# Loads of p and of two weights over other queues, and all steps in a new order

## Chip, core and metric

The kernel runs on one core of a Trainium2 chip. A core has five engines that each work through a list of instructions of their own, in order: TensorE (PE; its weight loads are listed as PEld), VectorE (DVE), ScalarE (ACT), GpSimd (POOL) and SyncE (SP), which only issues DMAs here. DMAs issued from SP, ACT and GpSimd go into queues that the same 16 DMA engines serve. The metric is the device time of one execution in microseconds. Before the change three runs gave a median of 108.91 us (108.64 to 110.49).

## What is computed

Two attentions through a packed set of 32 queries per head, and a token mixer behind them. B = 8 batches, H = 8 heads, S = 576 tokens, head width 64, D = 512; everything comes and goes in float32.

```python
def _attn_ref(q, k, v, p):
    def sm_attn(qq, kk, vv):
        s = scale * qq @ kk.T;  a = softmax(s)
        return a @ vv
    p_packed = sm_attn(p, k, v)           # 32 packed rows per head
    return sm_attn(q, p_packed, p_packed) # 576 rows per head

def _moe_ref(x, w_q, w_k, w_out):         # x: (8, 576, 512)
    wq = x @ w_q;  wk = x @ w_k           # 64 columns each
    W_tok = scale * einsum('bsd,btd->bst', wq, wk)
    mixed = einsum('bst,btd->bsd', W_tok, x)
    return maximum(mixed, 0) @ w_out
```

## The kernel before

Each batch goes through the same chain of steps, and the steps of several batches overlap. The program has no loops over time: `ORDER` is one long list of steps, written out, and since every engine runs its instructions in program order, the list fixes the order on each engine (and the order of the DMAs on each queue). A step is written `NAME.batch.part@engine=banks`: `@V`, `@A`, `@P`, `@S` choose VectorE, ScalarE, GpSimd or SyncE where a step can run on several; the numbers behind `=` are PSUM banks. Steps of TensorE carry no letter.

The loads, `LD.x` (`load`, lines 158 to 182): `LD.kN`, `LD.qN`, `LD.vN` bring in a batch's k, q, v from the GpSimd queue, float32 to bf16 on the way (v in two DMAs). `LD.g0` and `LD.h0` are the halves of batch 0's k. `LD.P0` to `LD.P3` are the four quarters of p, 32 partitions each, loaded in float32 into `p32`; `LD.W0`, `LD.W1` are w_q and w_k in float32; `LD.O` is w_out. k, q and v have four buffers each.

At the start: `SET.*` fill constants (line 190; `pz0` zeroes `pblk`, `v0` to `v3` write the columns of ones beside v, `warm` is the operand of the warm-up matmuls, `aT`, `mask`, `idf`, `aff`, `idb` are pads, a mask and the identity). `PC` (236) casts p to bf16, `PX` (239) transposes it, `PB.0.c` (243) copies a quarter into the block layout `pblk` that S1 of batches 0 and 1 reads. `WC.1`, `WC.0` (247) cast the weights. `WARM.n` runs n matmuls on a constant.

A batch b: `KT` (254) transposes k; `S1` (262) scores of p against k; `X1` (286) the exponential; `TE` (294) transposes it (batches 2 to 7); `PV` (299) times v and ones; `RC`, `PP`, `PT` (311 to 323) divide by the sum and transpose the packed rows; `QK` (325), `QKE`, `QD` put them through w_k and w_q; `QV.b.0/1/2` (345) transposes q in three pieces; `S2.b.c` (358) scores of q; `X2` (371) the exponential; `RS` (386), `RR` (392) sums and reciprocals; `AM.b.c` (397) multiplies, part 3 being 1024 columns and part 2 256; `AT`, `AE` (405, 412) transpose through PE and copy back; `WKQ`, `WE` (424, 447), `GM`, `GE` (452, 461), `Y`, `YE` (464, 472), `MX`, `MR` (479, 485) are the mixer; `RL`, `RLF`, `RLR` (506 to 515) the relu; `OT` (518) the last matmul with w_out, four parts of 512 columns and a part 4 for two batches' remaining rows; `OE`, `OEF` (536, 539) copy it out of PSUM; `ST`, `STF` (545, 563) store it from SP or ACT. `HOLD.q7` (557) is a tiny DMA on SP that waits for q7 and so keeps the stores behind it back. `HA` (381) adds the two halves of X2's result on GpSimd, so that RS has half as much to sum; no batch uses it before the change.

Names as in "S2.5" mean the step of batch 5.

Of the kernel before, what the change touches and what calls it, by code (L numbers as in the profile page):

```python
# [33 lines left out]
QKE.3@V QV.4.0@V RL.2.1@A LD.v5 LD.k6 AM.3.3@P QD.3@P LD.q6 PV.4.0=2,3 PV.4.1 RC.4.0@V RC.4.1@V
PP.4.0@V PP.4.1@V PT.4@V AT.3.3=6 RL.2.0@A OE.1.0@A AE.3.3@A AE.3.2@V OT.2.2=0,1 S2.4.2=2,3
S2.4.3=4,5 X2.4.2@A X2.4.3@A KT.5.2@V RS.4.4@V WKQ.3.0=6,7 WKQ.3.1 WKQ.3.2 OT.2.3 WE.3.2@A
S1.5=4,5,2,3 OT.2.0=6,7 OE.2.1@A RR.4.4@V GM.3=0 OT.2.1 X1.5.1@A X1.5.0@A GE.3@A AM.4.2@V Y.3=0
QK.4=4 AT.4.2=5 YE.3@A MR.3=0,1 MX.3.1=2,3 QKE.4@A RLR.3@A LD.v6 AM.4.3@P QD.4@P LD.k7 AT.4.3=4
OE.2.0@A RL.3.1@A QV.5.1@V TE.5.1@V TE.5.0@V QV.5.2@V PV.5.0=0,1 PV.5.1 QV.5.0@V AE.4.3@V
WKQ.4.0=6,7 AE.4.2@V RC.5.1@V RC.5.0@V WKQ.4.1 WKQ.4.2 PP.5.0@V PP.5.1@V MX.3.0=4,5 WE.4.2@A PT.5@V  # L40
RL.3.0@V S2.5.3=0,1 S2.5.2=2,3 GM.4=6 OT.3.4=7 X2.5.3@A GE.4@A X2.5.2@A Y.4=6 OEF.3.4@A QK.5=0
KT.6.2@V YE.4@V S1.6=2,3,4,5 RS.5.4@V OT.3.2=6,7 QKE.5@A X1.6.1@A X1.6.0@A MX.4.0=4,5 MX.4.1=0,1
MR.4=2,3 OT.3.3 QV.6.2@V TE.6.0@V RR.5.4@V TE.6.1@V QV.6.0@V QV.6.1@V LD.q7 LD.v7 QD.5@P AM.5.2@P
AM.5.3@P RLR.4@A RL.4.0@A RL.4.1@A OE.3.1@A OT.3.0=2,3 PV.6.0=4,5 PV.6.1 RC.6.0@V RC.6.1@V PP.6.0@V
PP.6.1@V OT.3.1 AT.5.3=0 PT.6@V S2.6.2=6,7 AE.5.3@V KT.7.2@V S2.6.3=4,5 OE.3.0@A X2.6.2@A X2.6.3@A
RS.6.4@V AT.5.2=1 AE.5.2@A OT.4.2=2,3 WKQ.5.0=6,7 S1.7=4,5,0,1 WKQ.5.1 WKQ.5.2 OT.4.3 X1.7.0@A
X1.7.1@A WE.5.2@A HOLD.q7 OT.4.0=4,5 OE.4.1@A GM.5=6 OT.4.1 RR.6.4@V AM.6.3@P AT.6.3=2 QV.7.1@V
TE.7.1@V TE.7.0@V AM.6.2@V QV.7.2@V AT.6.2=3 AE.6.3@V AE.6.2@V QV.7.0@V GE.5@A QK.6=6 Y.5=7
PV.7.0=0,1 PV.7.1 OE.4.0@A QKE.6@A YE.5@A QD.6@P MR.5=4,5 MX.5.1=6,7 RC.7.0@V RC.7.1@V RLR.5@A
WKQ.6.0=2,3 ST.1.4 ST.3.4 RL.5.1@A PP.7.0@V PP.7.1@V PT.7@V WKQ.6.2 WKQ.6.1 S2.7.2=0,1 WE.6.2@V  # L50
X2.7.2@A RS.7.2@V S2.7.1=4,5 MX.5.0=6,7 S2.7.0=0,1 GM.6=2 OT.5.4=3 X2.7.1@A X2.7.0@A GE.6@A Y.6=1
QK.7=2 RR.7.2@V AM.7.2@P AT.7.2=0 OEF.5.4@A QKE.7@A AE.7.2@A YE.6@A RL.5.0@V OT.5.0=6,7 MR.6=0,1
MX.6.1=4,5 MX.6.0=2,3 RLR.6@A RS.7.0@V RR.7.0@V RS.7.1@V RR.7.1@V AM.7.1@V RL.6.1@V AM.7.0@P QD.7@P
RL.6.0@A OT.5.1 OT.5.2=0,1 AT.7.0=2 AT.7.1=3 OT.6.0=4,5 AE.7.0@V AE.7.1@V OE.5.0@V WKQ.7.0=2,3
WKQ.7.2 WKQ.7.1 WE.7.1@A WE.7.0@V OT.5.3 OE.5.1@V GM.7=2 OT.6.1 GE.7@A ST.0.0 ST.0.1 ST.2.0 ST.1.1
ST.1.0 ST.4.0 ST.3.1 ST.3.0 ST.2.1 ST.4.1 ST.5.4 ST.5.0 OE.6.0@A ST.5.1 ST.6.0 Y.7=2 YE.7@V
OT.6.2=6,7 MX.7.1=0,1 MR.7=2,3 MX.7.0=4,5 RLR.7@V RLF.7.1.0@A RLF.7.1.1@A OT.6.3 OE.6.1@A
# [6 lines left out]
def kernel(  # L64
# [11 lines left out]
    nc = tc.nc  # L76
# [11 lines left out]
    B, H, S, Dh = q.shape  # L88
# [3 lines left out]
    P = 128  # L92
# [65 lines left out]
    def load(x, eng):  # L158
        a, b = x[0], x[1:]
        if a in "gh":  # L160
            i = "gh".index(a)
            nc.gpsimd.dma_start(k_in[0][:, i], pairs(k, 0)[:, i])
        elif a == "P":
            c = int(b)
            src = p.rearrange("b (i c) (y l) d -> c (b i) y (l d)", i=2, y=2)
            (nc.sync if eng == "S" else nc.scalar).dma_start(p32[quarter(c)], src[c])
        elif a == "W":
            w = (moe_w_q, moe_w_k)[int(b)].rearrange("(i c j e) m -> (c j) i (e m)", i=2, c=4, e=2)
            (nc.sync if eng == "S" else nc.scalar).dma_start(w32[:, int(b)].rearrange("a i e m -> a i (e m)"), w)
        elif a == "O":  # L170
            nc.gpsimd.dma_start(wout, moe_w_out.rearrange("(j a) n -> a j n", a=P))
        elif a == "v":
            b = int(b)
            for i in range(2):
                src = v[b, 4 * i:4 * i + 4].rearrange("c (g r) d -> g c (r d)", r=R)
                nc.gpsimd.dma_start(v_bufs[b % NL][halves(i), 1:5], src)  # L176
        elif a == "k":
            b = int(b)
            nc.gpsimd.dma_start(k_in[b % NL], pairs(k, b))  # L179
        else:  # L180
            b = int(b)
            nc.gpsimd.dma_start(q_in[b % NL], pairs(q, b))  # L182
# [40 lines left out]
    pbf = T["o"][NO - 4].rearrange("a t n -> a (t n)")[:, 0:L * Dh // 4].bitcast(bf16)  # L223
    warm = T["o"][NO - 5].rearrange("a t n -> a (t n)")[:, 0:256].bitcast(bf16)
    p32 = T["o"][NO - 1].rearrange("a t n -> a (t n)")[:, 0:L * Dh // 2]
# [8 lines left out]
        nc.vector.transpose(o, i)  # L234

    def PC(eng, bk):
        copy(eng, pbf, p32)

    def PX(eng, bk):
        blocks(pT.rearrange("a u (y l) e -> a (u y l e)", y=2).bitcast(u32).rearrange("a (u l) -> a l u", l=L // 2),  # L240
# [322 lines left out]
    def STF(b, t, eng, bk):  # L563
        q = nc.scalar if eng == "A" else nc.sync
        q.dma_start(orows(b)[:, :, t * D:(t + 1) * D], T["o", b][:, t])

    steps = dict(PC=PC, PX=PX, WC=WC, PB=PB, KT=KT, S1=S1, X1=X1, TE=TE, PV=PV, RC=RC, PP=PP,
                 PT=PT, QK=QK, QKE=QKE, QD=QD, QV=QV, S2=S2, X2=X2, HA=HA, RS=RS, RR=RR, AM=AM,
                 AT=AT, AE=AE, WKQ=WKQ, WE=WE, GM=GM, GE=GE, Y=Y, YE=YE, MX=MX, MR=MR, RL=RL, RLF=RLF,
                 RLR=RLR, OT=OT, OE=OE, OEF=OEF, ST=ST, STF=STF)  # L570

    with tc.manual_schedule():
        for item in ORDER.split():
            name, _, bk = item.partition("=")
            name, _, eng = name.partition("@")
# [43 lines left out]
```

## Time and profile before

One execution was profiled. Its time was 108.63 us; its span, from the first to the last instruction, is 106.9 us, and what lies around it is 1.73 us.

| | |
|---|---|
| median of three runs | 108.91 us |
| profiled run: time, span | 108.63, 106.9 us |
| granted TensorE clock, mean | 0.99 |
| TensorE busy | 95.9 us, 71 of 1535 matmuls are warm-up |
| VectorE, ScalarE, GpSimd busy | 79.3, 67.6, 44.3 us |
| GpSimd queue (q0): bytes, share of the 16 engines' span | 14.68 MB, 76.0% |
| output on SP (q1) | 9.44 MB, 22.9% |
| chain of waits: PE, DVE, DMA, ACT, POOL | 47, 19, 13, 7, 7% |

How to read it: the page gives busy sums, then the span cut into 40 slices of 2.67 us, where a digit is the busy share in tenths. A timeline row has the start, the duration, the engine, the line of the kernel, the operation, what it writes and reads with shapes, and in square brackets the idle time of the engine just before it and what ended it. "Time to landing" of a DMA runs from its issue to the semaphore that tells that all of it has arrived. A row of a table by stretch has, for each engine, the busy time in the stretch and the number of instructions, then the granted clock, the mean busy share of the DMA engines and GB/s. Bytes of the casting loads are counted at the destination, in bf16.

### The profile page before, as it was taken

The page shows a single profiled execution, that of the slowest core. Times are in us where ns is not written, and L with a number is a line of the kernel's source. Part 1 is how long each engine was busy: PE and PEld are TensorE (multiplying, and loading weights), DVE is VectorE, ACT ScalarE, POOL GpSimd, SP SyncE. Part 2 cuts the span into 40 slices and gives each one's busy share as a digit, 9 for nine tenths or more (in the row PEclk, how much of TensorE's full clock was granted, in tenths as well). Part 3 has the DMA queues.
Part 4 walks back from the last instruction along what each step waited for, and adds up shares of the span by engine and source line. Part 5 has one row for each costly group of instructions (what it writes and reads, how often), then busy time and mean ns, then how long its engine had stood idle before and what let it go on. Part 6 is the DMA issues. An engine that isn't in the chain of part 4 may idle for free.

```text
span 106.9 us, 3582 instructions
## 1 busy us (share of the span) xinstructions
PE 95.9 (90%) x1535; PEld 52.3 (49%) x1535; DVE 79.3 (74%) x158; ACT 67.6 (63%) x106; POOL 44.3 (41%) x63
## 2 busy tenths in 40 slices
PE   5999197899999999999999999999999999999930
PEld 2344064564735564645466446645657653643410
DVE  5040709769999979896998899999998999986000
ACT  2334041450684469977999979889978788057840
POOL 6995324539459523920465098019024126000000
PEclk9999999999999999999999999999999999999996
DMA  1899999999999999999999999999999999657694
GB/s 38 205 175 195 214 217 210 210 213 213 205 210 210 206 208 214 213 214 202 212 216 206 215 206 210 211 211 207 175 381 402 408 408 400 272 205 311 244 376 157
DMA packets 13215, 25.13 MB, mean 235 GB/s; under 512 B 1040, under 2 KB 6160, under 8 KB 13200
## 3 DMA queue, kind: packets, MB, share of 16 engines
q0 software_dynamic: 9248, 14.68, 76.0%
q1 hardware_dynamic: 3168, 9.44, 22.9%
q10 hardware_dynamic: 784, 0.79, 2.8%
q8 instruction: 12, 0.20, 0.7%
q14 instruction: 3, 0.02, 0.1%
HBM read 30.15 MB, written 9.44 MB: 370 GB/s over the span
## 4 chain that ended last, share of the span: by engine, by line
PE 47%; DVE 19%; DMA 13%; ACT 7%; POOL 7%; issue 3%; DVEq 0%; ACTq 0%; POOLq 0%
PE ps L531 23%; DMA k_sb<-in_k_dram 13%; PE ps L369 5%; DVE qT L234 3%; PE ps L483 3%; PE ps L308 3%; DVE pp L317 3%; DVE rs L390 3%; ACT relu L494 2%; POOL a L401 2%; DVE aT L135 2%; PE ps L458 2%; PE ps L410 2%; PE ps L586 2%; PE ps L281 2%
## 5 line engine op out<-in xcount | busy, mean ns | idle before, releaser
L531 PE MATMUL ps<-wout,relu 128*128 128x512 bf16 x128 | 31.7, 380 | 0.0
L401 POOL TENSOR_TENSOR a<-e,rr 128x1024 bf16<-128x1024 f32 (+2 forms) x12 | 15.8, 1320 | 23.9 <-DVE rr L395 15.2
L586 PE MATMUL ps<-o 128*128 128x512 bf16 x71 | 19.8, 418 | 1.2 <-DVE o L138 1.2
L531 PEld LDWEIGHTS <-relu 128*128 128x128 bf16 x128 | 11.1, 98 | 11.7 <-issue 1.5
L131 ACT ACTIVATE o<-ps 128x1024 f32<-128x1024 f32 (+1 forms) x16 | 14.8, 922 | 2.3 <-PE ps L531 2.2
L374 ACT ACTIVATE e<-ps 128x256 f32<-128x256 f32 (+2 forms) x17 | 10.9, 671 | 8.0 <-PE ps L369 7.7
L494 ACT ACTIVATE relu<-ps 128x1024 bf16<-128x1024 f32 (+1 forms) x12 | 14.3, 1236 | 1.1 <-PE ps L489 0.5
L234 DVE STREAM_TRANSPOSE qT<-q_sb 128x512 uint32<-128x512 uint32 (+1 forms) x24 | 12.6, 550 | 2.6 <-DMA q_sb<-in_q_dram 2.6
L234 DVE STREAM_TRANSPOSE kT<-k_sb 128x1152 uint32<-128x1152 uint32 (+1 forms) x9 | 11.1, 1235 | 3.9 <-DMA k_sb<-in_k_dram 3.9
L390 DVE TENSOR_REDUCE rs<-e 128x40 f32<-128x1280 f32 (+2 forms) x10 | 12.0, 1201 | 2.0 <-ACT e L374 2.0
L586 PEld LDWEIGHTS <-o 128*128 128x128 bf16 x71 | 6.7, 106 | 9.8 <-issue 3.6
L176 POOL DMA_DIRECT2D v_sb<-in_v_dram x16 | 10.3, 651 | 1.7 <-DMA k_sb<-in_k_dram 1.2
L131 ACT ACTIVATE wkq<-ps 128x896 bf16<-128x896 f32 (+1 forms) x7 | 6.0, 864 | 5.0 <-PE ps L437 5.0
L234 DVE STREAM_TRANSPOSE e<-e1T 128x576 bf16<-128x576 bf16 x12 | 8.4, 735 | 0.0
L369 PE MATMUL ps<-ppT,qT 64*128 64x64 bf16 x320 | 6.8, 190 | 1.7 <-DVE ppT L234 1.1
L292 ACT ACTIVATE e1T<-ps 128x576 bf16<-128x576 f32 x12 | 7.3, 652 | 1.4 <-PE ps L281 1.3
L308 PE MATMUL ps<-v_sb,e 64*64 64x192 bf16 x288 | 7.8, 245 | 0.4 <-ACT rem L494 0.3
L369 PEld LDWEIGHTS <-qT 64*128 64x128 bf16 x320 | 5.9, 94 | 4.6 <-issue 1.8
L179 POOL DMA_DIRECT2D k_sb<-in_k_dram x7 | 5.1, 731 | 7.0 <-DMA k_sb<-in_k_dram 4.2
L182 POOL DMA_DIRECT2D q_sb<-in_q_dram x8 | 5.8, 730 | 3.4 <-DMA q_sb<-in_q_dram 2.2
L308 PEld LDWEIGHTS <-e 64*64 64x64 bf16 x288 | 6.1, 106 | 2.3 <-ACT e L289 1.0
L410 PE MATMUL ps<-idb,a 128*128 128x128 bf16 x80 | 6.9, 220 | 0.3 <-POOL a L401 0.2
(64 smaller groups left out, 133.8 us busy)
## 6 DMA issues: line engine op xcount, KB each, us to landing
out_dram<-o SPq DMA_DIRECT2D x14, 512.0 KB, 6.3
v_sb<-in_v_dram POOLq DMA_DIRECT2D x16, 288.0 KB, 14.7
q_sb<-in_q_dram POOLq DMA_DIRECT2D x8, 576.0 KB, 16.3
k_sb<-in_k_dram POOLq DMA_DIRECT2D x7, 576.0 KB, 16.7
out_dram<-orem SPq DMA_DIRECT2D x4, 256.0 KB, 3.2
out_dram<-o SPq DMA_DIRECT2D x3, 256.0 KB, 2.9
k_sb<-in_k_dram POOLq DMA_DIRECT2D x2, 288.0 KB, 7.6
wout<-in_moe_w_out_dram POOLq DMA_DIRECT2D x1, 512.0 KB, 18.4
```

What stands on the lines that cost most here:

```text
L131: nc.scalar.activation(o, i, COPY)
L176: nc.gpsimd.dma_start(v_bufs[b % NL][halves(i), 1:5], src)
L234: nc.vector.transpose(o, i)
L308: nc.tensor.matmul(T["pv", b][halves(cc), i, cc * Dh:(cc + 3) * Dh], lhsT, rhs, start=n == 0, stop=n == R - 1, skip_group_check=True)
L369: nc.tensor.matmul(ps[:, y, t - t0, i], lhsT, rhs, start=e == 0, stop=e == 1)
L374: nc.scalar.activation(e2[:, t0:t1].rearrange("a t (i y n) -> a y (t i) n", i=2, y=2), T["s2", b, c].rearrange("a y t i n -> a y (t i) n") ...
L390: nc.vector.tensor_reduce(rs[:, t0 * H:t1 * H], src, axis=AX, op=ADD)
L401: e.tensor_tensor(a2[:, t0:t1].rearrange("a t i (u l) -> a (t i u) l", l=L), e2v(b, c), T["rr", b][:, t0 * H:t1 * H].to_broadcast((P, (t1 ...
L410: nc.tensor.transpose(ps[:, i, t - t0], T["a2", b][:, t, i], idb)
L494: nc.scalar.activation(o, i, RELU)
L531: nc.tensor.matmul(ps, lhsT, wout[:, j, :], start=j == 0, stop=j == NJ - 1)
L586: nc.tensor.matmul(ps, warm[:, 0:P], warm, start=True, stop=True)
```

## The change

Three things.

p comes over three queues. P1 is issued from SP and P0 from ACT, one each, in float32 as before. P2 and P3 are issued from GpSimd and cast on the way, straight into the bf16 buffer `pbf`; `PC` casts only the other 64 partitions. On the GpSimd queue the order is now g0, P2, h0, P3, v0, where it was v0, g0, h0.

Both weights are issued from SP, right behind P1; they were issued from ACT, behind PC and behind two of the PB steps.

All 515 steps but one are the same, in a new order, with other PSUM banks, and some on another engine; HA.5 is new. Warm-up matmuls are 78, not 71.

```diff
         elif a == "P":
             c = int(b)
             src = p.rearrange("b (i c) (y l) d -> c (b i) y (l d)", i=2, y=2)
-            (nc.sync if eng == "S" else nc.scalar).dma_start(p32[quarter(c)], src[c])
+            if c > 1:
+                nc.gpsimd.dma_start(pbf[quarter(c)], src[c])
+            else:
+                (nc.sync if eng == "S" else nc.scalar).dma_start(p32[quarter(c)], src[c])
...
     def PC(eng, bk):
-        copy(eng, pbf, p32)
+        copy(eng, pbf[0:64], p32[0:64])
```

The order, at its beginning, where the next loads follow, and around HA.5:

```diff
-LD.P0@S SET.pz0@P SET.v0@P LD.P2@A LD.P3@A LD.P1@S LD.v0 SET.warm@V SET.aT0@V SET.aT1@V SET.v1@V
-SET.tab@A PC@A SET.mask@V PX@V SET.aT2@V LD.g0 KT.0.0@V PB.0.1@V SET.v2@P LD.h0 LD.q0 SET.idf@V
-KT.0.1@V LD.k1 LD.v1 LD.q1 QV.0.1@V QV.0.2@V QV.0.0@V LD.k2 LD.W1@A PB.0.2@A PB.0.0@A LD.W0@A
-PB.0.3@A WARM.34=3 S1.0=0,1,2 X1.0.0@A SET.aff@P LD.v2 LD.q2 WC.1@P WARM.5=3 PV.0.0=0,1 PV.0.1
...
-MR.4=2,3 OT.3.3 QV.6.2@V TE.6.0@V RR.5.4@V TE.6.1@V QV.6.0@V QV.6.1@V LD.q7 LD.v7 QD.5@P AM.5.2@P
-AM.5.3@P RLR.4@A RL.4.0@A RL.4.1@A OE.3.1@A OT.3.0=2,3 PV.6.0=4,5 PV.6.1 RC.6.0@V RC.6.1@V PP.6.0@V
...
+LD.P1@S LD.P0@A SET.aT2@V SET.aT1@V SET.idf@V SET.pz0@V SET.warm@V SET.tab@A SET.v0@V SET.v1@V LD.g0
+LD.P2 LD.h0 LD.P3 LD.W1@S LD.W0@S PC@A LD.v0 SET.aff@P SET.v3@P PX@V KT.0.1@V SET.v2@V LD.q0
+SET.mask@P PB.0.0@A KT.0.0@V WC.1@V PB.0.2@V PB.0.1@A PB.0.3@A LD.k1 WARM.33=3 S1.0=0,1,2 X1.0.0@A
+WARM.5=3 PV.0.0=0,1 PV.0.1 SET.idb@V SET.aT0@V QV.0.1@V QV.0.0@V RC.0.1@V RC.0.0@V QV.0.2@V PP.0.1@V
+PP.0.0@V PT.0@V WARM.12=2 S2.0.2=6,7 S2.0.3=0,1 X2.0.2@A X2.0.3@A WC.0@P LD.v1 LD.q1 KT.1.2@V LD.k2
+WARM.4=2 S1.1=5,6,7 X1.1.0@A WARM.5=0 PV.1.0=6,7 PV.1.1 QK.0=1 LD.q2 RS.0.4@V RR.0.4@V AM.0.3@P
+LD.v2 RC.1.1@V RC.1.0@V QKE.0@A LD.k3 LD.O QD.0@P PP.1.0@V PP.1.1@V AM.0.2@V QV.1.0@V QV.1.2@V
...
+OE.3.1@A RL.4.0@A HA.5@P LD.q7 RS.5.4@V TE.6.0@V RR.5.4@V TE.6.1@V AM.5.2@P AM.5.3@P LD.v7 QD.5@P
```

Steps on another engine up to batch 6: off VectorE RL.0.1, RL.3.0, RLR.0, AE.0.3, AE.2.3, AE.4.2, QKE.2, QKE.3, YE.2, WE.6.2 (to ACT) and AM.2.3 (to GpSimd); onto VectorE AM.0.2, AM.2.2 (from GpSimd), YE.0, YE.1, GE.1, GE.3, GE.4, RLR.1, RLR.2, QKE.5, OEF.1.4, WE.4.2, RL.5.1, YE.6 (from ACT). In batch 7 AM.7.2, AM.7.0 and RLF.7.1.0, RLF.7.1.1 come to VectorE; AM.7.1 goes to GpSimd; RLF.7.0.0, RLF.7.0.1, AE.7.0 and YE.7 go to ACT. The relus of batch 7 thus swap engines, and WE.7.0 and WE.7.1, OE.5.0 and OE.6.0 swap as well. The list of the stores on SP is ST.3.4, ST.3.1, ST.1.4, ST.4.1, ST.0.0 and so on behind HOLD.q7; it was ST.1.4, ST.3.4, ST.0.0.

## The prediction

> **What bounds the kernel now.** I read the busy shares and the slices of the page first, then the timeline of VectorE, the sums by stretch, and last the DMA issues one by one.
>
> ```profile
> PE 95.9 (90%) x1535; PEld 52.3 (49%) x1535; DVE 79.3 (74%) x158; ACT 67.6 (63%) x106; POOL 44.3 (41%) x63
> ...
> DVE  5040709769999979896998899999998999986000
> ACT  2334041450684469977999979889978788057840
> ...
> DMA  1899999999999999999999999999999999657694
> ```
>
> The 16 DMA engines are full from 5 us to about 77 us: the inputs come as one unbroken stream. VectorE is full only from about 27 us. So two stages: first loads decide, later compute. The timeline of VectorE shows the first stage:
>
> ```profile
> 15.87 1.50 DVE L234 STREAM_TRANSPOSE qT<-q_sb 128x512 uint32<-128x512 uint32 x3 [2.57 <-DMA q_sb<-in_q_dram]
> ...
> 19.25 1.38 DVE L234 STREAM_TRANSPOSE kT<-k_sb 128x1152 uint32<-128x1152 uint32 x1 [0.51 <-DMA k_sb<-in_k_dram]
> ...
> 27.72 1.38 DVE L234 STREAM_TRANSPOSE kT<-k_sb 128x1152 uint32<-128x1152 uint32 x1 [0.16 <-DMA k_sb<-in_k_dram]
> ```
>
> QV.0, KT.1 and KT.2 each start within 0.03 us of their load's landing (15.85, 19.22, 27.70: issue plus time to landing, load by load). Afterwards compute falls behind: k4 lands at 47.25 and KT.4 starts at 47.70, k6 64.47 and 67.60, k7 72.92 and 75.96, v7 78.93 and PV.7 at 82.24. The lag of 3.3 us at v7 is all that a better order can win back before the tail, beyond what the stream itself gains. By stretches:
>
> ```profile
> core 0: us, PE busy (x) PEld busy (x) DVE busy (x) ACT busy (x) POOL busy (x), PEclk, DMA share, GB/s
> ...
> 40.00:50.00 10.00, 9.58 (x157) 5.48 (x145) 8.64 (x15) 8.19 (x12) 4.40 (x7) 1.00 1.13 211
> 50.00:60.00 10.00, 9.86 (x206) 5.41 (x204) 9.14 (x18) 9.63 (x15) 4.50 (x5) 1.00 1.15 210
> 60.00:70.00 10.00, 9.62 (x219) 5.82 (x202) 9.70 (x19) 8.71 (x16) 5.12 (x7) 1.00 1.15 211
> 70.00:80.00 10.00, 9.90 (x169) 5.35 (x167) 9.56 (x18) 8.85 (x13) 3.07 (x3) 1.00 1.08 245
> 80.00:90.00 10.00, 9.61 (x181) 5.73 (x180) 9.36 (x21) 8.15 (x18) 3.56 (x5) 1.00 1.02 402
> ```
>
> Three engines are near full together; ACT bounds 50 to 60 us (9.63 of 10), VectorE 60 to 70.
>
> **The front.** The loads. Now the first GpSimd load is issued at 2.08 us and its first packet runs at 3.78, 1.70 later. LD.g0 would be the first real GpSimd work, at 0.73, so packets at 2.43. The work of the DMA engines up to q0 stays about the same, so only their idle time can be won: the busy shares are 0.79, 1.10, 0.63 and 1.11 in the four microseconds from 2 to 6, which leaves 0.58. Bounds: 0 to 1.35 (2.08 less 0.73); I take **-0.6**: q0 lands at 15.25, k1 18.6, k2 27.1.
>
> P2 and P3 as casting loads have no row. Nearest: half of k, 128 packets of 193 ns; at that price 32 packets are 0.39 us on 16 engines. Engine time up to P3: g0 and h0 3.1, P2 and P3 0.8, P0 and P1 (64 packets of 246 ns) 1.0, both weights (512 of 39 ns) 1.25, so 6.1 from about 2.2: done by 8.3. Landing adds 0.3 (v7's last packet 78.60, landed 78.93) to 1.2 (h0), so PX starts at 8.6 to 9.5. Then on VectorE, before PB.0.2: PX 1.04, KT.0.1 0.78, v2 0.54, mask 0.7 (SET.mask@P is written with nc.vector, so it runs on VectorE), KT.0.0 0.78, WC.1 about 0.3, PB.0.2 0.22: 4.4 in all. S1.0 starts at 13.0 to 13.9 (13.35 now), PV.0 ends by 17.3. RC.0 stands behind QV.0.1 and QV.0.0, which wait for q0 and end at 16.5, so the cover is q0's landing; gone, it costs up to 0.8. PE's warm-up starts later, with warm behind pz0 on VectorE, and ends about 11.5, still ahead.
>
> The weights land 8.3 and 9.4 us after issue now, beside a full queue 0; p's quarters 2.9 to 4.2. Issued at about 1.5 and 1.9 they land between 4.4 and 11.3. WC.1 comes up on VectorE at about 12; WC.0 holds LD.v1, LD.q1, LD.k2 and LD.q2 on GpSimd till 11.7 at most, and v1's packets are due only when k1's end, about 18. Both free, as are the four issues that ACT loses. AM.0.3, now ahead of LD.v2, LD.k3 and LD.O, ends at about 23.8 (RR.0 21.9 plus 1.91); v2 is due when q2's packets end, about 29.5. Free; cover 4 us.
>
> **The middle.** Off VectorE go RL.0.1 and RL.3.0 (2 x 1.29), RLR.0 0.41, AE.0.3 and AE.2.3 (2 x 0.68), AM.2.3 1.18, QKE.2 and QKE.3 (2 x 0.40), YE.2 0.40, AE.4.2 0.21: 6.9. Onto it: AM.0.2 and AM.2.2 (2 x 0.45), YE.0, YE.1 and QKE.5 (3 x 0.40), RLR.1 and RLR.2 (2 x 0.41), WE.4.2 1.05, OEF.1.4 (rows of 0.61 and 0.72: 0.65), three GE (0.21 to 0.34: 0.28): 5.5. RS.5 reads half as much: 0.77 for 1.47 (rows 0.42, 0.65, 1.47 for 256, 512, 1280). VectorE is 2.1 lighter up to batch 5, ACT some 2.4 heavier. Followed step by step in the new order with the timeline's spacings:
> - KT.2 27.65 (27.72 now): QV.1.0, QV.1.2, PT.1 and QV.1.1 run to 26.55, then S2.1.3 0.65, behind it AT.0.2 0.25, then AE.0.2 0.2, which now stands ahead of KT.2. The stream's 0.6 is lost here.
> - KT.3 36.45 (37.62): KT.2 1.36, RS.1 1.45, RR.1 0.40, QV.2 1.44, YE.0 0.40, TE.2 1.39, AE.1 0.85, RC, PP and PT 1.33, and 0.2 of waiting for Y.0.
> - KT.4 47.6 (47.70): KT.3, GE.1 and YE.1 to 38.8, RS.2 from 39.1 (X2.2.2 is late) 1.45, then TE.3.1, RR.2, AM.2.2, RLR.1, TE.3.0 2.65, PV.3 0.95, RC to PT 1.35, QV.3 1.44, OEF.1.4 0.65. k4 has landed at 46.65.
> - X2.3.2 48.1 (48.70). From it to the end of X2.4.3 ACT takes 10.33 now, with 0.22 idle; new: QKE.3 and YE.2 in, OEF.1.4 and RLR.2 out, -0.2, less what new waits give back. X2.4.3 ends at 58.5 (59.03): VectorE's relief is not what counts there.
> - KT.6 67.15 (67.60): RS.4 to 59.95, GE.3, RR.4, QV.5.1, TE.5.1 to 61.95, TE.5.0 from 62.15 (X1.5.0) to 62.85, AM.4.2 0.44, QV.5.0 0.62, AE.4.3 0.65, QV.5.2 0.20, RC to PT 1.33, WE.4.2 1.05. X2.5.2 ends at 68.2 (68.74).
> - HA.5, a 128x640 add on GpSimd, lies between 1.05 (512 columns) and 1.91 (1024); I take 1.25. It ends at 69.5, then RS.5 0.77, TE.6.0 0.70, RR.5 0.40 and 0.2 of waits: 71.6 (71.94).
> - KT.7 75.8 (75.96): TE.6.1 0.70, QV.6 1.44, RC to PT 1.35, AE.5.3 0.65. PV.7 follows on PE behind AT.6.2, Y.5 and QK.6; AM.6.2 ends at 81.5 (KT.7 1.36, RS.6 1.45, RR.6 0.40, TE.7 1.40, QV.7.0 0.62, AM.6.2 0.44), so PV.7 is ready for all but v7 at 82.1 (82.24).
>
> Seven more warm matmuls (78 for 71) are 1.5 us of PE at 0.21, in gaps before 40 us: free.
>
> **The last load** is what HA.5 and the order on GpSimd touch. Now:
>
> ```profile
> 63.66 0.76 POOL L179 DMA_DIRECT2D k_sb<-in_k_dram  x1
> 64.41 0.73 POOL L182 DMA_DIRECT2D q_sb<-in_q_dram  x1
> 65.13 1.27 POOL L176 DMA_DIRECT2D v_sb<-in_v_dram  x2
> ```
>
> New, LD.q7 waits behind HA.5 (69.5; k7's packets last to about 72, so no hole), and LD.v7 behind AM.5.2 and AM.5.3 (2.48 for the two): 71.6 + 2.5 = 74.1, nine microseconds later than now, first packet 75.8. 512 packets of 109 ns are 3.5 us: last packet 79.3. But HOLD.q7 lets the stores go once q7 has landed, about 75.1, and ST.3.4, ST.3.1 and ST.1.4 have 2.7 us of packets (128 x 86, 167 and 86 ns over 16). Turn by turn v7 lands at 79.6 + 2.7 = 82.3, just when PV.7 is ready. How queues share:
>
> ```profile
> q0 software_dynamic: 324, 0.70, 91.4%
> q10 hardware_dynamic: 317, 0.15, 19.0%
> ```
>
> (the DMA view from 10 to 14 us): one weight packet for one load packet. The Trainium skill (DMA: Bandwidth & Descriptors, Queues, rings and completion order) has each DMA engine go round-robin between the queue rows that have work, a packet at a time. The trace agrees (324 to 317). By it v7 lands at 82.3, by age alone at 79.6.
>
> **The tail.** From PV.7 PE is full (9.6 of 10, then 7.00 of 7.00). The output work is the same. RL.5.1 and RL.5.0 both stand on VectorE ahead of RS.7.2 (2 x 1.29, against WE.6.2 1.05 and one RL now), so AM.7.0, after PT.7 at 84.5, 2.6 for these, 4.1 for RS.7, RR.7, YE.6, AM.7.2 and itself, ends about 91.2 (AM.7.0 and AM.7.1 at 89.72 and 90.26 now) and holds AT.7.0 some 0.5; WKQ.7 then goes ahead of OT.6.0, which gives that back. Bounds -1 to +1, from these two; taken 0.
>
> Sum: PV.7 starts at 82.1 or, by v7, at 82.3, so between -0.1 and 0.1; with the 0.5 that X2.5.2 still leads by, of which I count a half, and a tail of 0, the end moves by -0.2. Span 106.7 and 1.73 around it (108.63 less 106.9, the profiled run): **108.4**. The median of three is 108.91, 0.28 above that run.
>
> **Rivals.**
> - *Lead kept* (24%). VectorE, not ACT, sets the middle, so its 2.1 counts in full with the 0.6 of the stream: 108.63 - 2.7 = 105.9. For: VectorE 9.70 and 9.56 of 10 at 60 to 80 us. Against: ACT at 9.63.
> - *v7 late* (30%). PV.7 stands in PE's order and everything behind it waits. It decides once v7 lands after 82.3, and each microsecond is paid whole, as PE has none to spare behind it. HA.5 at its upper bound +0.7, a fourth store (ST.4.1) ahead +1.3, landing 1.2 after the last packet, as at h0, instead of 0.3: +0.9. All of them: 108.4 + 2.9 = 111.3. For: nine microseconds of cover are given up. Against: ST.4.1 may still wait for its operand.
> - *Front late* (4%): P3 or a weight after q0's cover, +0.8: 109.2.
> - *Washes out* (42%), the forecast; its own range 106.9 to 110.4: the tail's bounds of 1 each way, and on the upper side another 1 for waits that such a walk can't see, and 0.5 on the lower for the front's bound.
>
> **Numbers.** About 2% (2.2 us, so 106.7 and 111.1) is what a measurement can tell from no change. Faster: most of the first rival (0.20) and 0.02 of the forecast, 0.22. Slower: 0.18 of the second, as not all its parts must come together, and 0.10 of the forecast, whose walk errs to the short side: 0.28. Within: 0.50. The range runs from the first rival to the second with half a microsecond over it, 105.9 to 111.8.
>
> **What would show it.** k2 landing near 27.1 (stream); KT.3 near 36.5; X2.4.3 ending by 58.5; v7 landing against PV.7's start: equal or later is *v7 late*. Wrong if S1.0 starts after 14, if the DMA slices show a hole before 70 us, or if PE idles over 1 us ahead of AT.7.0.

## The result and the profile after

The changed kernel takes 110.35 us (median of four runs, 110.11 to 112.05) against 108.99 for the kernel before: a ratio of 1.0128 with a 95% interval of 1.0083 to 1.0174. That is inside the 2% that counts as no change, but it is a loss, and the prediction of 108.4 saw a small gain. The medians in this document are over all runs, while the ratios, by which the runs are judged, leave out runs in a slower state, into which the first profiles of two kernels below (the two halves) fell, so that no positions are taken from them. The profiled run took 110.19 us with a span of 108.42; before, the span was 106.86, so 1.56 us are to be found.

The page's busy shares and slices, and the sums by stretch, of the changed kernel:

```profile
PE 97.1 (90%) x1542; PEld 53.3 (49%) x1542; DVE 79.0 (73%) x163; ACT 70.4 (65%) x105; POOL 44.8 (41%) x62
...
DMA  1999999999999999999999999949799999939992
```

```profile
core 0: us, PE busy (x) PEld busy (x) DVE busy (x) ACT busy (x) POOL busy (x), PEclk, DMA share, GB/s
40.00:50.00 10.00, 9.92 (x174) 5.35 (x174) 8.53 (x17) 9.01 (x13) 5.59 (x7) 1.00 1.13 210
50.00:60.00 10.00, 9.90 (x185) 5.69 (x184) 8.66 (x18) 9.66 (x14) 4.33 (x5) 1.00 1.15 211
60.00:70.00 10.00, 9.69 (x231) 5.80 (x230) 9.63 (x19) 8.63 (x14) 3.67 (x4) 1.00 1.13 210
70.00:80.00 10.00, 9.89 (x170) 5.42 (x167) 9.33 (x18) 8.46 (x12) 5.51 (x7) 1.00 0.80 121
```

The middle looks as before: three engines near full, ScalarE at 9.66 of 10 from 50 to 60 us (9.63 before). New are holes in the transfers at 70 to 73 us and a lesser one behind 76. The hole at 95 to 97 us is deeper than any in the tail before, which had four slices in a row at 0.5 to 0.7.

The front is where the profile differs. The timeline of VectorE, with the steps QV.0, RC.0, KT.1, and then AE.0.2 and KT.2:

```profile
14.61 1.31 DVE L237 STREAM_TRANSPOSE qT<-q_sb 128x512 uint32<-128x512 uint32 x2 [0.89 <-DMA q_sb<-in_q_dram]
16.99 0.35 DVE L316 RECIPROCAL rec<-ps 64x2 f32<-64x2 f32 x2 [1.07 <-PE ps L311]
...
18.31 1.34 DVE L237 STREAM_TRANSPOSE kT<-k_sb 128x1152 uint32<-128x1152 uint32 x1
...
28.76 0.23 DVE L135 COPY aT<-ps 128x128 bf16<-128x128 bf16 x1 [0.98 <-PE ps L413]
28.90 1.38 DVE L237 STREAM_TRANSPOSE kT<-k_sb 128x1152 uint32<-128x1152 uint32 x1
```

The loads come earlier than before: k1 lands at 17.75 (19.22 before), k2 at 26.09 (27.70). But KT.1 and KT.2 no longer start when their load lands. KT.2 starts 2.8 us after k2 has landed, and 1.18 later than before. VectorE waits for TensorE instead: 1.07 us for PV.0 and 0.98 for AT.0.2. The chain of waits, in order of time (start, length, what), names what TensorE was doing:

```profile
3.05 6.00 DMA o<-in_p_dram
9.18 1.04 DVE pT L237
...
15.91 0.94 PE ps L311 x36
16.84 2.70 PE ps L589 x12
19.54 0.72 PE ps L372 x40
```

The load of P3 is the first long piece; PX starts behind it. Between PV.0 (L311) and S2.0 (L372) stand 2.70 us of warm matmuls (L589), in the chain that ended last. PT.0 was done at 18.38, so S2.0 could have started some 1.1 us before 19.47 (its first matmul on TensorE's timeline). VectorE's 1.07 us for PV.0 therefore did not hold S2.0. RC.0 at 16.99 was still 0.41 ahead of the kernel before (17.40), where S2.0 did wait for PT.0, as TensorE's timeline of before shows for PV.0, the warm matmuls and S2.0:

```profile
15.80 0.94 PE L308 MATMUL ps<-v_sb,e 64*64 64x192 bf16 x36
16.67 1.47 PE L586 MATMUL ps<-o 128*128 128x512 bf16 x6
18.79 0.78 PE L369 MATMUL ps<-ppT,qT 64*128 64x64 bf16 x40 [0.65 <-DVE ppT L234]
```

So between PT.0 and S2.0 a lead of 0.36 us turned into a lag of 0.68.

The last loads, in GpSimd's own timeline:

```profile
69.25 1.55 POOL L387 TENSOR_TENSOR h<-e 128x640 f32<-128x640 f32 x1 [4.32 <-ACT e L377]
70.75 0.74 POOL L185 DMA_DIRECT2D q_sb<-in_q_dram  x1
72.78 2.48 POOL L404 TENSOR_TENSOR a<-e,rr 128x256 bf16<-128x256 f32 x2 [1.29 <-PE ps L534]
75.22 1.29 POOL L179 DMA_DIRECT2D v_sb<-in_v_dram  x2
```

q7 and v7 go out late, hence the hole in the transfers, but v7 lands at 81.11 and PV.7 starts only at 82.99: nothing waits for it.

From PV.7 on, the 1.56 us divide thus: PV.7 starts 0.75 later (82.99 for 82.24); TensorE's work from PV.7 to its last matmul takes 20.66 for 20.33; from there to the end of the span, 4.76 for 4.29. So about half is lost before PV.7 and half behind it.

### The profile page after: what moved, and what is told of

The parts are those of the page before. It is cut to its first block, busy times and chain, and to the rows that moved or that the text cites. A ratio compares the mean times of both kernels' runs of the same rounds, so it can differ in the third digit from the quotient of the medians.

```text
span 108.4 us, 3591 instructions
## 1 busy us (share of the span) xinstructions
PE 97.1 (90%) x1542; PEld 53.3 (49%) x1542; DVE 79.0 (73%) x163; ACT 70.4 (65%) x105; POOL 44.8 (41%) x62
## 4 chain that ended last, share of the span: by engine, by line
PE 51%; DVE 29%; DMA 6%; issue 4%; POOL 3%; ACT 3%; DVEq 0%; ACTq 0%; POOLq 0%
PE ps L534 20%; PE ps L589 6%; DMA o<-in_p_dram 6%; PE ps L372 5%; DVE qT L237 4%; PE ps L311 4%; DVE pp L320 3%; DVE rs L393 3%; PE ps L413 3%; DVE kT L237 2%; DVE a L404 2%; DVE relu L499 2%; PE ps L274 2%; PE ps L486 2%; DVE e L237 2%
## 5 line engine op out<-in xcount | busy, mean ns | idle before, releaser
L589 PE MATMUL ps<-o 128*128 128x512 bf16 x78 | 21.2, 415 | 2.0 <-DVE o L138 2.0
L497 ACT ACTIVATE relu<-ps 128x1024 bf16<-128x1024 f32 (+1 forms) x13 | 15.6, 1236 | 1.9 <-PE ps L486 0.9
L589 PEld LDWEIGHTS <-o 128*128 128x128 bf16 x78 | 7.4, 105 | 11.0 <-issue 3.0
L393 DVE TENSOR_REDUCE rs<-e 128x40 f32<-128x1280 f32 (+2 forms) x9 | 10.6, 1175 | 3.0 <-ACT e L377 3.0
L237 DVE STREAM_TRANSPOSE e<-e1T 128x576 bf16<-128x576 bf16 x12 | 8.9, 756 | 0.4 <-ACT e1T L295 0.3
L133 POOL COPY pqk<-pqk 128x128 bf16<-128x128 bf16 x8 | 2.5, 309 | 14.1 <-ACT pqk L131 14.1
L372 PE MATMUL ps<-ppT,qT 64*128 64x64 bf16 x320 | 6.9, 190 | 1.0 <-DVE ppT L237 0.7
L311 PE MATMUL ps<-v_sb,e 64*64 64x192 bf16 x288 | 7.6, 245 | 0.1
L413 PE MATMUL ps<-idb,a 128*128 128x128 bf16 x80 | 6.8, 220 | 0.8 <-DVE a L404 0.5
L372 PEld LDWEIGHTS <-qT 64*128 64x128 bf16 x320 | 5.9, 94 | 3.2 <-issue 1.7
L311 PEld LDWEIGHTS <-e 64*64 64x64 bf16 x288 | 6.0, 106 | 2.2 <-ACT e L292 1.1
L413 PEld LDWEIGHTS <-a 128*128 128x128 bf16 x80 | 4.8, 98 | 4.2 <-POOL a L404 2.3
```

The source lines that it names most:

```text
L311: nc.tensor.matmul(T["pv", b][halves(cc), i, cc * Dh:(cc + 3) * Dh], lhsT, rhs, start=n == 0, stop=n == R - 1, skip_group_check=True)
L372: nc.tensor.matmul(ps[:, y, t - t0, i], lhsT, rhs, start=e == 0, stop=e == 1)
L393: nc.vector.tensor_reduce(rs[:, t0 * H:t1 * H], src, axis=AX, op=ADD)
L413: nc.tensor.transpose(ps[:, i, t - t0], T["a2", b][:, t, i], idb)
L497: nc.scalar.activation(o, i, RELU)
L589: nc.tensor.matmul(ps, warm[:, 0:P], warm, start=True, stop=True)
```

## The experiments

Each was timed beside the kernel before on one chip. A start in a single profile moves with the first loads' landing, so positions are compared as distances: PV.0 to KT.2, PV.0 to PV.7, PV.7 to the end of the span.

| run | median us | ratio to before (95%) | PV.0 | PV.0 to KT.2 | PV.7 | PV.7 to end |
|---|---|---|---|---|---|---|
| before (profile) | 108.91 | | 15.80 | 11.92 | 82.24 | 24.62 |
| changed | 110.35 | 1.0128 (1.0083 to 1.0174) | 15.91 | 12.99 | 82.99 | 25.43 |
| changed, again | 110.10 | 1.0113 (1.0063 to 1.0162) | 16.26 | 12.84 | 83.09 | 25.44 |
| new front, old order | 108.82 | 0.9992 (0.9955 to 1.0028) | | | | |
| old front, new order | 109.18 | 1.0031 (0.9991 to 1.0071) | 15.58 | 12.84 | 81.96 | 25.33 |
| five warm matmuls | 110.16 | 1.0104 (1.0016 to 1.0191) | 16.53 | 11.80 | 82.37 | 25.44 |
| the same, AT.0.2 earlier | 109.04 | 1.0024 (0.9983 to 1.0065) | 16.11 | 10.71 | 81.44 | 25.43 |
| q7, v7 early | 112.32 | 1.0269 (1.0188 to 1.0349) | 16.12 | 12.83 | 83.81 | 25.43 |
| without HA.5 | 112.38 | 1.0281 (1.0210 to 1.0352) | 16.17 | 12.99 | 83.75 | 26.90 |
| ST.4.0 earlier | 109.94 | 1.0071 (1.0039 to 1.0104) | 16.75 | 12.99 | 83.73 | 25.06 |
| AM.7.2 later | 109.95 | 1.0062 (1.0036 to 1.0088) | 16.49 | 12.84 | 83.32 | 25.14 |
| four repairs | 108.17 | 0.9894 (0.9860 to 0.9928) | 15.93 | 10.83 | 81.28 | 24.78 |
| p as before | 108.83 | 0.9982 (0.9956 to 1.0008) | 14.92 | 12.84 | 81.41 | 25.31 |
| p as before, four repairs | 107.21 | 0.9825 (0.9788 to 0.9861) | 15.12 | 11.52 | 80.75 | 24.65 |

For "old front, new order" the positions are those of its second profile.

**Halves of the change.** The changed kernel with its front up to S1.0, then before's order; and the front of before up to S1.0, then the new order:

```diff
 (changed: loads, constants, PX ... S1.0=0,1,2)
-(the changed kernel's steps behind S1.0)
+(the steps of before behind S1.0, those already done left out)
```

> The changed front (loads of p and of the weights, set-up, all steps up to S1.0), and behind S1.0 every step in the order of before. Theory 'the order behind the front loses it': in the changed kernel k2 lands 1.6 us earlier (26.09 for 27.70) but KT.2 starts 1.2 later (28.90 for 27.72); with the old order KT.2 starts within 0.3 us of k2's landing, so near 26.2, and the end is 0.5 to 1.5 us earlier than before, 107.4 to 108.4. Rival 'compute bounds from 28 us on, whenever the loads come': KT.2 is early, but the end is that of before within 0.4 us. Rival 'the loads do harm': 109.5 or more.

> The other half: the front of before up to S1.0, and behind it the steps in the new order. Theory 'the order behind the front loses it': S2.0 waits for the twelve warm matmuls and starts near 19.4, KT.2 near 28.9, and the time is that of the changed kernel or up to 0.5 above it, 110.2 to 110.9. Rival 'the loads do harm': about 109.0.

Neither half alone can be told from the kernel before: 108.82 and 109.18 us. My theory, that the front wins and the order behind it loses, falls in both; the rivals' numbers are near. The loss takes both halves. The changed kernel itself, run again, kept it:

> The changed kernel itself, unaltered, once more, next to the three below on one chip. If the 1.3% is the program's own, it gives 110.0 to 110.7 us again, a ratio of 1.010 to 1.017 to the kernel before. If the loss was a matter of the chip or of the moment, it lies within 0.5% of the kernel before, as the two halves of the change did.

It gave 110.10. So what the order loses is paid only with the new front, or the front's loss only with the new order. The second half was profiled once more, for its positions:

> The front of before up to S1.0 with the new order behind it, once more, for its profile alone, since the first one had a stretch of low TensorE clock. It came out at 109.18 us, though it has the twelve warm matmuls and the late AT.0.2 too. If the warm matmuls hold S2.0.2 only because PV.0 ends where the new front puts it, they end before PT.0 here, S2.0 starts within 0.3 of PT.0's end, and KT.2 starts at 27.8 to 28.3, below the changed kernel's 28.9. If KT.2 is at 28.9 or later all the same, the delay is made good behind it, and KT.2 does not set the end: PV.7 would then be at or below 82.3 with a late KT.2.

KT.2 came at 28.42, PV.7 at 81.96. Neither expectation holds cleanly: the warm matmuls stand in front of S2.0 here too (16.45 to 19.2), and PV.0 to KT.2 takes 12.84, the same as in the repeated run of the changed kernel, although RC.0 here does not wait for PV.0 at all. What the old front moves on this stretch is the start of PV.0, 15.58.

**The warm matmuls and AT.0.2.**

```diff
-PP.0.0@V PT.0@V WARM.12=2 S2.0.2=6,7
+PP.0.0@V PT.0@V WARM.5=2 S2.0.2=6,7
```

> The changed kernel with 5 warm matmuls ahead of S2.0 instead of 12. In the changed kernel PT.0 ends at 18.38 and S2.0 starts at 19.47, when the twelve are done. Theory 'the early delay is carried to the end': S2.0 starts near 18.5, KT.2 near 28.0, and the end comes 0.7 to 1.0 us earlier, 109.3 to 109.6. Rival 'the middle absorbs it': KT.2 as said, but KT.5 within 0.3 us of 57.44 and the end within 0.3 us of the changed kernel.

```diff
-WARM.2=0 AT.0.3=5 AE.0.3@A WARM.4=6 QK.1=0 S2.1.3=6,7 AT.0.2=5 AE.0.2@V
+WARM.2=0 AT.0.3=5 AT.0.2=4 AE.0.3@A WARM.4=6 QK.1=0 S2.1.3=6,7 AE.0.2@V
```

> The changed kernel with five warm matmuls for twelve ahead of S2.0.2, and AT.0.2 right behind AT.0.3, ahead of QK.1 and S2.1.3 as before, in bank 4. Theory (KT.2's delay of 1.2 us is made by these two, and is carried to the end): KT.2 starts at 27.2 to 27.8, PV.7 at 81.7 to 82.3, time 108.9 to 109.4. Rival (only the warm matmuls count, as in the run with five alone, or compute catches up): KT.2 earlier, but PV.7 not below 82.3, time 109.4 to 109.8.

The second run has both edits. VectorE's timeline at KT.2, first with five warm matmuls alone, then with AT.0.2 ahead of QK.1 and S2.1.3 as well:

```profile
28.19 0.23 DVE L135 COPY aT<-ps 128x128 bf16<-128x128 bf16 x1 [0.99 <-PE ps L413]
28.33 1.37 DVE L237 STREAM_TRANSPOSE kT<-k_sb 128x1152 uint32<-128x1152 uint32 x1
```

```profile
26.12 0.67 DVE L237 STREAM_TRANSPOSE qT<-q_sb 128x512 uint32<-128x512 uint32 x1
26.71 0.18 DVE L135 COPY aT<-ps 128x128 bf16<-128x128 bf16 x1
26.82 1.36 DVE L237 STREAM_TRANSPOSE kT<-k_sb 128x1152 uint32<-128x1152 uint32 x1
28.82 1.49 DVE L393 TENSOR_REDUCE rs<-e 128x40 f32<-128x1280 f32 x1 [0.64 <-ACT e L377]
```

The reader sees the wait for TensorE (L413) ahead of KT.2 vanish. From PV.0 to KT.2 each edit is worth 1.0 to 1.2 us (12.99 or 12.84 without them, then 11.80 and 10.71). With five alone, TensorE's timeline has S2.0 waiting for PT.0 again:

```profile
17.40 1.25 PE L589 MATMUL ps<-o 128*128 128x512 bf16 x5
19.06 0.78 PE L372 MATMUL ps<-ppT,qT 64*128 64x64 bf16 x40 [0.41 <-DVE ppT L237]
```

It starts 2.53 us behind PV.0 in each of the three kernels with five and the casting loads. With twelve it starts 3.56 or 3.57 behind PV.0 in all eight profiles of this document that have them, whenever p comes: there TensorE's order sets it, not PT.0.

The edit of AT.0.2 meets a new wait behind KT.2, 0.64 for ScalarE's X2.1, so that from PV.0 to PV.7 the two together bring 1.75 (67.08 to 65.33; 1.50 from the repeated run's 66.83), and in time 1.1 (110.10 to 109.04, both on one chip). In time the five warm matmuls alone can't be told from the changed kernel: their ratio, 1.0104, has an interval of 1.0016 to 1.0191, though the profile moved as expected. The stretch behind PV.7 stays at 25.4 in both: the tail's loss is a matter of its own.

**The last loads.**

```diff
-AM.4.3@P LD.k7 QD.4@P AT.4.3=0
+AM.4.3@P LD.k7 LD.q7 LD.v7 QD.4@P AT.4.3=0
```

> The changed kernel with the loads of q7 and v7 issued right behind that of k7, ahead of HA.5 and of AM.5. Theory 'v7 is not what PV.7 waits for' (in the changed kernel v7 lands at 81.11 and PV.7 starts at 82.99): the hole in the DMA stream at 70 to 73 and 76 us is gone, q7 lands near 74.5 and v7 near 78, and the end is within 0.3 us of the changed kernel. Rival 'v7 late': PV.7 and the end come 0.5 us or more earlier.

With a ratio of 1.0269 it is slower still, and part of that is a fault of my edit, which the timelines of GpSimd and of TensorE show:

```profile
64.69 0.73 POOL L185 DMA_DIRECT2D q_sb<-in_q_dram  x1
65.41 1.27 POOL L179 DMA_DIRECT2D v_sb<-in_v_dram  x2
66.63 0.33 POOL L133 COPY pqk<-pqk 128x128 bf16<-128x128 bf16 x1
```

```profile
67.03 0.39 PE L440 MATMUL ps<-aT,pqk 128*128 128x256 bf16 x2 [0.84 <-POOL pqk L133]
```

Two microseconds of issuing stand ahead of QD.4, WKQ.4 waits 0.84 for it, and KT.5 to KT.6 takes 11.47 for 10.50. The rest of the loss I did not trace. The run prices an issue ahead of a due step, and says nothing for or against v7. The next one does, though it was made for HA.5:

```diff
-OE.3.1@A RL.4.0@A HA.5@P LD.q7 RS.5.4@V
+OE.3.1@A RL.4.0@A LD.q7 RS.5.4@V
```

> The changed kernel without HA.5, so that RS.5 adds all 1280 columns again. Theory (the halving add costs more than it saves, because VectorE waits for GpSimd): HA.5 took 1.55 us from X2.5.2's end, and RS.5 then 0.82; without it RS.5 takes 1.47 from the same end, so RR.5 comes 0.9 earlier (71.4 for 72.26), q7 and v7 land up to 1.5 earlier, and the hole in the transfers is gone. Of the 0.9 between 0 and 0.9 reaches PV.7: 109.3 to 110.3. Rival (HA.5 is a gain or hidden): RR.5 not earlier than 72.1, the time unchanged or up to 0.5 longer.

The theory falls, and the time is 2 us longer. First RS.5, with HA.5 (the changed kernel) and without it, in VectorE's timelines:

```profile
70.83 0.82 DVE L393 TENSOR_REDUCE rs<-h 128x40 f32<-128x640 f32 x1 [0.18 <-POOL h L387]
```

```profile
70.83 1.48 DVE L393 TENSOR_REDUCE rs<-e 128x40 f32<-128x1280 f32 x1
```

VectorE is busy until 70.65 with other steps, so all but 0.18 of HA.5 is hidden, and leaving it out makes RS.5 longer: KT.7 comes 0.45 later than in the repeated run (77.30 for 76.85). HA.5 is a small gain. The larger part of the loss is a wait of TensorE in the middle of PV.7:

```profile
83.75 0.24 PE L311 MATMUL ps<-v_sb,e 64*64 64x192 bf16 x1
85.75 0.93 PE L311 MATMUL ps<-v_sb,e 64*64 64x192 bf16 x35 [1.75 <-DMA v_sb<-in_v_dram]
```

```profile
q0 software_dynamic: 540, 0.59, 51.4%
q1 hardware_dynamic: 521, 1.28, 37.6%
```

The first fence is TensorE's timeline, the second the queues from 76 to 85 us (packets, MB, share). Without HA.5 ahead of it q7 is issued at 65.12 instead of 70.75 and lands at 75.77 instead of 76.69, so HOLD.q7 lets the stores go 0.92 sooner; v7, behind AM.5 and the longer RS.5, leaves 0.64 later. The first store now goes out at 76.42, between the two halves of v7 (75.86 and 76.53). Loads and stores take turns, 540 packets to 521, and v7's second half needs 9.18 us to land; in the changed kernel, where the first store leaves 1.46 us behind it, 5.23. This is the rival *v7 late*, as a mechanism: true, and in the changed kernel 1.9 us away from counting. The Trainium skill (DMA: Bandwidth & Descriptors, Queues, rings and completion order) has a DMA engine go round-robin between queues by packets; 540 to 521 agrees.

**The tail.**

```diff
-ST.3.0 ST.5.4 ST.1.1 ST.2.0 ST.5.0 ST.1.0 ST.5.1 ST.4.0 ST.6.0
+ST.3.0 ST.5.4 ST.1.1 ST.2.0 ST.4.0 ST.5.0 ST.1.0 ST.5.1 ST.6.0
```

(the list of stores without what stands between them)

> The changed kernel with the store ST.4.0 moved on SyncE ahead of ST.5.0; it stood behind ST.5.1, which waits for OE.5.1 until 96.35 us, while its own rows had long been ready. Theory (the queue of stores is still full at the end, and part of the tail's loss is there): the hole in the transfers at 92 to 96 us takes these 512 KB, the last store lands 2.5 instead of 2.82 us after its issue, PE unchanged; 109.6 to 109.9 us beside 110.1 to 110.3 of the changed kernel. Rival (the last store's own latency, whatever is queued): the same 2.8, no change.

```diff
-RS.7.0@V AM.7.2@V RR.7.0@V AM.7.0@V
+RS.7.0@V RR.7.0@V AM.7.0@V AM.7.2@V
```

> The changed kernel with AM.7.2 on VectorE moved behind AM.7.0; it took 1.01 us right ahead of it, and TensorE waited 0.55 for AM.7.0 ahead of AT.7.0, while AT.7.2 comes only after OT.5.3. Theory: AM.7.0 ends at 91.3 instead of 92.3, the 0.55 is gone or below 0.1, and the end comes 0.3 to 0.55 earlier: 109.6 to 109.9. Rival (the gap only moves, to AT.7.2 or to OT.5.3): a new idle time of 0.3 or more behind it, no change.

Both moved what they were made to move. In the changed kernel VectorE's timeline shows AM.7.2, RR.7.0 and AM.7.0, GpSimd's AM.7.1, and TensorE's AT.7.0 waiting:

```profile
90.42 1.01 DVE L404 TENSOR_TENSOR a<-e,rr 128x256 bf16<-128x256 f32 x1
91.35 0.24 DVE L398 RECIPROCAL rr<-rs 128x16 f32<-128x16 f32 x1
91.63 0.69 DVE L404 TENSOR_TENSOR a<-e,rr 128x512 bf16<-128x512 f32 x1
```

```profile
90.10 1.05 POOL L404 TENSOR_TENSOR a<-e,rr 128x512 bf16<-128x512 f32 x1 [0.72 <-DVE rr L398]
```

```profile
92.38 0.40 PE L413 MATMUL ps<-idb,a 128*128 128x128 bf16 x4 [0.55 <-DVE a L404]
```

With AM.7.2 moved, both products on VectorE and all eight transposes on TensorE:

```profile
91.15 1.21 DVE L404 TENSOR_TENSOR a<-e,rr 128x512 bf16<-128x512 f32 x2
```

```profile
91.77 0.70 PE L413 MATMUL ps<-idb,a 128*128 128x128 bf16 x8
```

The 0.55 is gone, a wait of 0.17 appears behind it, and from PV.7 to TensorE's last matmul it takes 20.37 instead of 20.66. With ST.4.0 moved, the last store lands 2.52 us after its issue instead of 2.82, and PV.7 to the end is 0.37 shorter. In time (109.94 and 109.95) both are just above what was expected (109.6 to 109.9), and each interval overlaps that of the unchanged run: the traces show these two gains, the times alone do not.

A splice of the changed order up to PV.7 with the tail of before was run too, at 111.79 us. That program computes something else, and I did not trace which step it loses, so nothing is read from its time or profile.

**All four repairs.**

> The four repairs together: five warm matmuls for twelve, AT.0.2 ahead of S2.1.3, ST.4.0 ahead of ST.5.0, AM.7.2 behind AM.7.0. Theory (the new middle is as good as the plan meant it, and the loss lay in two places of the front and two of the tail): PV.7 at 81.3 to 81.7 as with the first two alone, the stretch behind it 24.5 to 24.8, time 107.7 to 108.2, a ratio of 0.988 to 0.994 to the kernel before. Rival (what the front gains is taken back in the tail): 108.4 to 109.0, a ratio of 0.997 to 1.003.

The time, 108.17 us, is at the upper edge of the theory's range and the ratio, 0.9894, inside it, below 1 with its whole interval. In the profiles, 110.19 becomes 107.84; PV.7 comes 1.71 earlier and the stretch behind it is 0.65 shorter, together 2.36. Of the 0.81 us that the changed kernel lost behind PV.7, 0.16 is left.

**p as before.** What the old front had that the new one lacks was still open. In every profile with the casting loads that is used here P3 lands at 9.05 to 9.89 us and PX starts 0.13 later; in the kernel before PX started at 6.93. The profile of the changed kernel itself had the earliest P3 of all.

```diff
-            if c > 1:
-                nc.gpsimd.dma_start(pbf[quarter(c)], src[c])
-            else:
-                (nc.sync if eng == "S" else nc.scalar).dma_start(p32[quarter(c)], src[c])
+            (nc.sync if eng == "S" else nc.scalar).dma_start(p32[quarter(c)], src[c])
...
-LD.P1@S LD.P0@A ... LD.g0 LD.P2 LD.h0 LD.P3 LD.W1@S
+LD.P1@S LD.P3@S LD.P0@A LD.P2@A ... LD.g0 LD.h0 LD.W1@S
```

with PC casting all of p again.

> The changed kernel with P2 and P3 loaded as before (float32, P2 from ScalarE's queue behind P0, P3 from SyncE's behind P1, PC casting all 128 partitions); weights behind them on SyncE and the whole new order unchanged. In every profile so far with the two casting loads, PX starts 0.13 after P3's landing, which lay at 9.05 to 9.9 us, and PV.0 6.7 to 7.0 after PX (15.9 to 16.75); with p as before PX started at 6.9 to 7.3. Theory (P3 sets the front, so part of the loss is the three queues for p): PX at 6.8 to 7.6, KT.0.1 then waits for h0 instead, PV.0 at 14.8 to 15.6, and the rest of the program 0.4 to 1.0 earlier: 109.2 to 109.9. Rival (k1 and k2 set the pace from KT.1 on, and the time between is slack): PV.0 earlier, KT.2 still 0.2 or less below its 28.9 to 29.1, time 110.0 to 110.5.

> The same with the four repairs (five warm matmuls, AT.0.2, ST.4.0, AM.7.2), which gave 108.17 with the casting loads. Theory (P3 sets the front): PV.0 at 14.8 to 15.6, KT.2 at 26.1 to 26.6, where k2's landing ends what can be won, 107.4 to 107.9. Rival (slack): KT.2 at 26.7 to 27.0 and 108.0 to 108.4.

VectorE's timeline, PX and RC.0, with p as before and the new order unchanged, and below it TensorE's, PV.0 and S2.0:

```profile
8.14 1.04 DVE L234 STREAM_TRANSPOSE pT<-o 128x512 uint32<-128x512 uint32 x1 [4.95 <-ACT o L131]
...
16.01 0.35 DVE L313 RECIPROCAL rec<-ps 64x2 f32<-64x2 f32 x2 [0.15 <-PE ps L308]
```

```profile
14.92 0.94 PE L308 MATMUL ps<-v_sb,e 64*64 64x192 bf16 x36
...
18.48 0.78 PE L369 MATMUL ps<-ppT,qT 64*128 64x64 bf16 x40
```

PX is later than I expected (8.14, behind the cast on ScalarE, which ends at 8.11), but PV.0 is at 14.92 as expected, and VectorE's wait for it ahead of RC.0 has shrunk from 1.07 to 0.15. That wait is not where the gain lies: S2.0 is at 18.48, again 3.56 behind PV.0 and 1.08 behind the end of PT.0, so what counts is that PV.0 itself is 0.99 earlier than in the changed kernel (1.34 earlier than in its repeated run). The time is 108.83 us, a ratio of 0.9982 where the repeated run of the changed kernel had 1.0113, and better than the theory's range. In this order, then, the casting loads of p alone cost as much as the whole loss. With the four repairs it is 107.21 us, 1.75% below the kernel before, and the best version here; the casting loads are worth about half as much there (a ratio of 0.9894 to 0.9825). KT.2 there is at 26.64, 0.03 behind the landing of k2 (26.61), and VectorE's step ahead of it ends at 26.59: the front has come up to the loads again.

## Why the prediction was wrong

Its direction was wrong by one step of the front, the twelve warm matmuls taken as free, and by the tail, taken as 0. The walk through the middle held.

- *The stream, -0.6.* Too small: k1 came 1.47 and k2 1.61 earlier. It bought nothing, since KT.2 started 2.8 us after k2.
- *PX 8.6 to 9.5, S1.0 13.0 to 13.9; "the cover is q0's landing; gone, it costs up to 0.8".* PX at 9.18 and S1.0 at 13.43 are right. The cover did go: the same change that made p late made q0 early, QV.0.1 and QV.0.0 were done at 15.9 and not at 16.5, and RC.0 waited 1.07 for PV.0. But this wait, which *front late* (4%) was priced by, reached nothing, as PT.0 was still done ahead of S2.0. Late p was paid on TensorE, by the next item; restoring its loads alone took the ratio from 1.0113 to 0.9982, so *front late* deserved far more than 4%, for another reason than the one it gave.
- *"Seven more warm matmuls ... in gaps ... free".* This is the step that failed. They stand in TensorE's order, and the twelve ahead of S2.0, where there were six, end 1.1 us after PT.0. They cost S2.0 1.03 us against five (3.56 behind PV.0 for 2.53), and they tie it to PV.0, so that each delay of p comes through whole. I counted how many there were and not where. None of the signs that the prediction named for being wrong stood at S2.0: S1.0 started before 14, the first hole in the transfers came behind 70 us, and TensorE idled 0.55 ahead of AT.7.0.
- *KT.2 27.65.* It was 28.90. The wait for AT.0.2 was in the walk, and the run without it shows it to be worth 1.1. What was missing is that QV.1.1 ended at 27.8 rather than 26.55, behind PV.1, behind S1.1 and the late S2.0.
- *The middle.* From KT.2 to KT.3 8.80 was forecast and 9.01 measured, KT.3 to KT.4 11.15 and 11.02, KT.4 to KT.6 19.55 and 19.01, KT.6 to KT.7 8.65 and 8.72, KT.7 to PV.7 6.3 and 6.33. So the start error of 1.25 was carried to PV.7 nearly whole (0.89). *Lead kept* was rightly doubted: with VectorE's relief, KT.2 to PV.7 takes 54.09, against 54.52 before.
- *HA.5, 1.25.* It took 1.55, and hardly counted, as VectorE reached RS.5 only 0.18 before its end.
- *v7 at 82.3.* It landed at 81.11; the stores came 1.46 us behind v7's second half, not beside the whole of it. *v7 late* (30%) is a real mechanism, but with a margin of 1.9.
- *The tail, 0 from bounds of 1 each way.* It was +0.81. The 0.5 ahead of AT.7.0 was foreseen (0.55), but "WKQ.7 ... gives that back" was at least half wrong: with the wait gone, TensorE's work from PV.7 on was 0.29 shorter. AM.7.2, taken from rows near 0.45, took 1.01 beside GpSimd. And the stores' order was read only at v7, not at the end.

What stays open: with p as before, or with the whole old front, the way from PV.0 to PV.7 is also 0.3 to 0.7 shorter (66.49 and 66.38, for 67.08 and 66.83). One piece is AM.4.2, which takes 0.56 beside GpSimd's AM.4.3 and 0.38 where they don't meet; the rest I did not trace. Why before's order pays nothing for the late p stays open as well. It has six warm matmuls ahead of S2.0 and not twelve, and before the change its S2.0, KT.1 and KT.2 waited for q0's steps and for loads, but no profile used here shows that order with the new front.

## What to carry over

Filler matmuls are work in an ordered queue: price each block by the moment at which the step behind it could start. A block that ends later than that ties the step behind it to the step ahead of it, and whatever delays the one is then paid whole by the other, whatever cover there is on another engine. An idle time is a cost only if something behind it waits: RC.0's 1.07 us was plain to see in the changed kernel, and nothing hung on it. In a walk through a steady pipeline, intervals were good to a few tenths and the starting point was not, so check the first 30 us twice, and read the tail by who waits on TensorE and which store stands behind an unready one.

## What the runs showed of the hardware

- *VectorE's product waits for GpSimd's.* AM, with two operands in SBUF, started on VectorE while GpSimd's AM was running, ends 0.28 us after GpSimd's does for 256 columns (AM.7.2 at 91.43 for 91.15, AM.4.2 at 64.20 for 63.92, and before the change AM.6.2 at 81.60 for 81.32). One that started within 0.02 us of GpSimd's did not wait: AM.3.2 before the change took 0.41, and GpSimd's product 2.19 for the usual 1.91. Most rows without a GpSimd product beside them take 0.38 to 0.43 (two of AM.0.2 take 0.54); AM.7.2 took 1.01. The Trainium skill (SBUF — State Buffer, SBUF: two separate sides) calls the ports that the two engines share an exclusive lock, which the loser waits for; the rows agree.
- *A store issued between the two halves of a load nearly doubles the second's time to landing*, 9.18 us for 5.23, as the two queues take turns.
- *Casting loads of p on GpSimd's queue landed later* than float32 loads on the other queues: P3 at 9.05 to 9.89, 6.00 to 6.84 us after its issue; p's last quarter in float32 at 5.74 to 7.20, 4.25 to 5.70 after its issue. P3 stands behind three other loads on its queue and the float32 quarter behind one, so the runs do not tell the cast from the place in the queue.
